# Tiles 4 to 7 normed in quarters and transposed by VectorE, with the scales spread by one masked product for four tiles

## The chip, the cores and the metric

One core of a Trainium2 chip runs the whole program. The metric is device time in microseconds (us), of whole executions; beside it one execution was taken by the hardware profiler, and its span, its rows and its waits are what the texts below read. PE is TensorE, ACT is ScalarE, DVE is VectorE, POOL is GpSimd, and SP (SyncE) issues the DMAs.

## The reference

x has 2048 rows of 640. Its rows are normed to mean 0 and variance 1, and the normed xn goes two ways:

```python
xn = _layernorm(x, axis=-1)
s = _A_ref(xn, A_wqkv, A_wo)          # 32 heads of 20; each row attends to 8 rows, 2 apart
g = _silu(_B_ref(xn, B_w_gate, B_w_up, B_w_down))   # ((xn Wg) * (xn Wu)) Wd, width 1536
return x + s * g
```

## The kernel before

The rows are cut into 16 tiles of 128 partitions. Tile s holds every 16th row, and tiles 0 to 7 are the even columns, 8 to 15 the odd ones, so that the dilated window of a row lies in neighbouring tiles of the same parity. All products are done in three passes of a fast fp32 type: each operand is split into a high part (a copy by ACT) and a low part (raw minus high, by DVE or POOL), and `mm3` adds high·high, high·low and low·high.

The order of the work is written out by hand: each engine executes its instructions in the order in which the program issues them, and waits at an instruction until its operands and its buffers are free. The stages are:

1. **Norming and transposing x** (to about 70 us). The products need xn with its 640 columns on the partitions, in `xT`: four chunks of four tiles, each with a high and a low part. `moments` gives mean and variance of a tile (two bn_stats and one bn_aggr on DVE), `rstd` the reciprocal root (Sqrt on ACT, L191, then a Newton step on DVE, L194 to L206), `apply` the normed tile (L209).
   - Tiles 0 to 7: `norm`, then `trans` (L223): five 128x128 transposes on PE against the identity, a high copy by ACT from PSUM (L224) and two low parts by DVE (L225).
   - Tiles 8 to 15: `moments` reads the tile as it lies; then the tile is loaded again (`load_xq`) from `xq`, a layout prepared on the host in which the 32-row and 160-column blocks are already exchanged, so that a transpose within 32x32 blocks, which DVE can do, finishes the job. In that layout a partition holds four quarters that belong to four different rows. Therefore the scales have to be spread: `spread` multiplies the table of means and scales of eight tiles (`mro`) by four selection matrices (`sel`, L240), and ACT copies the result out of PSUM (`mrq`, L241). `trans_odd` then applies four quarters (L209), transposes (L249), lets ACT make the high part (L252) and leaves the low part (L254) to be done behind the next tile's transpose, or by `low_parts`.
2. **Units and gate_ups** (to about 560 us). A unit u is a group of heads at one parity: `qkv(u, i)` is the product of tile i of that parity by the unit's weights, in one of four PSUM banks of tag q, copied by ACT into `q_t` and `kv_t` (L289, L290). Two kv buffers alternate. When a unit's eight blocks are done, `attention(u)` joins the list `running`. It is a generator; `advance` takes as many of its steps as a credit of estimated DVE time allows, and `drain(u - 2)` takes all that is left before unit u begins. Its steps are pairs of product and sum for the logits (L321, L324), the softmax with an exponent on ACT (L333), weighted sums (L342, L350, L353). `gate_up(f, ch)` is a block of 128 gate columns by chunk ch: a half g and a half u, 15 products each, in PSUM tags g and u with two banks each. ACT copies g to `gs` (L389). Then, while attention is running, DVE multiplies u by gs (L400), issued amid the next piece; while none is running, ACT copies u (L402) and POOL multiplies (L403), at once. An h_scr DMA stores the result. Units 0 and 1 and gate_ups (0, 0) to (1, 3) are written out singly (L650 to L700); from unit 2 on, three or four gate_ups follow each unit.
3. **Output projection, then the down projection** with a Strassen-like scheme and the gated sum (from about 560 us).

The weights of a gate block are split in the same way, the high part by ACT (L85), the low part by POOL (L86), one block ahead.

The order of the program around the change, from about 20 us on: qkv(0, 2), qkv(0, 3), second part of gate_up(0, 0), transposes of tiles 4 and 5, gate_up(1, 0) with the transposes of tile 6 between its halves, those of tile 7, qkv(0, 4), qkv(0, 5), gate_up(0, 1) with the spread between its halves, qkv(0, 6), qkv(0, 7), gate_up(1, 1), unit 1 (eight blocks), gate_up(0, 2), (1, 2), (0, 3), (1, 3), unit 2.

Of the kernel before, what the change touches and what calls it, by code (L numbers as in the profile page):

```python
# [13 lines left out]
AF = mybir.ActivationFunctionType  # L14
# [5 lines left out]
P = 128  # L20
S, D, F = 2048, 640, 1536
H, DH = 32, 20
W, DIL = 8, 2
NT = S // P
NE = NT // DIL
# [4 lines left out]
TPC = CH // P  # L30
# [4 lines left out]
QB = 32  # L35
NQ = P // QB
QC = D // NQ
# [13 lines left out]
def kernel(  # L51
# [11 lines left out]
    nc = tc.nc  # L63
# [11 lines left out]
    def st(shape, tag, bufs, dt=F32):  # L75
        cnt[0] += 1
        return sb.tile(shape, dt, tag=tag, bufs=bufs, name=f"{tag}_{cnt[0]}")

    def pt(shape, tag, bufs):
        cnt[0] += 1  # L80
        return ps.tile(shape, F32, tag=tag, bufs=bufs, name=f"{tag}_{cnt[0]}")
# [37 lines left out]
    def load_wf(f):  # L119
        wf_raw[f] = st([P, KD, 2, P], "wraw", 3)  # L120
        nc.sync.dma_start(wf_raw[f], wgu[f])
# [8 lines left out]
    xt = {}  # L130
# [15 lines left out]
    xc = st([P, NE, D], "xc", NCH)  # L146
# [5 lines left out]
    ident = st([P, P], "ident", 1)  # L152
# [27 lines left out]
    def moments(s0, n, mv=None):  # L180
        stats = st([P, n, 2, 6], "stats", 2)
        mv = st([P, n, 2], "mv", 2) if mv is None else mv
        for i in range(n):
            for a in range(2):
                nc.vector.bn_stats(stats[:, i, a, :], xt[s0 + i][:, a * HALF:(a + 1) * HALF])
            nc.vector.bn_aggr(mv[:, i, :], stats[:, i])
        return mv

    def rstd(var, out, n):
        r = st([P, 4, NE], "rstd", 2)[:, :, :n]  # L190
        nc.scalar.activation(r[:, 0, :], var, AF.Sqrt, bias=eps_t)  # L191
        step = 1 if n <= 2 else n
        for i in range(0, n, step):
            nc.vector.tensor_scalar_add(r[:, 1, i:i + step], var[:, i:i + step], EPS)  # L194
        nc.vector.reciprocal(r[:, 2, :], r[:, 0, :])
        if step == 1:
            for i in range(n):
                ve, a, b = (r[:, k, i:i + 1] for k in (1, 2, 3))
                nc.vector.tensor_scalar(b, a, a, ve, op0=ALU.mult, op1=ALU.mult)
                nc.vector.tensor_scalar(b, b, -0.5, 1.5, op0=ALU.mult, op1=ALU.add)  # L200
                nc.vector.tensor_scalar(out[:, i:i + 1], b, a, None, op0=ALU.mult)
            return
        nc.vector.tensor_mul(r[:, 3, :], r[:, 2, :], r[:, 2, :])
        nc.vector.tensor_mul(r[:, 3, :], r[:, 3, :], r[:, 1, :])
        nc.vector.tensor_scalar(r[:, 3, :], r[:, 3, :], -0.5, 1.5, op0=ALU.mult, op1=ALU.add)
        nc.vector.tensor_mul(out, r[:, 3, :], r[:, 2, :])  # L206

    def apply(y, m, r):
        nc.vector.tensor_scalar(y, y, m, r, op0=ALU.subtract, op1=ALU.mult)  # L209

    def norm(s0, n, mv=None):
        mv = moments(s0, n) if mv is None else mv
        r = st([P, n], "r", 2)
        rstd(mv[:, :, 1], r, n)
        for i in range(n):
            apply(xt[s0 + i], mv[:, i, 0:1], r[:, i:i + 1])

    def trans(s):
        hi, lo = xT_tile(s)
        for k0, k1 in ((0, 4), (4, KD)):  # L220
            p = pt([P, k1 - k0, P], "q", 4)
            for k in range(k0, k1):
                nc.tensor.transpose(p[:, k - k0, :], xt[s][:, k * P:(k + 1) * P], ident)  # L223
            nc.scalar.activation(hi[:, k0:k1, :], p, AF.Copy)  # L224
            nc.vector.tensor_sub(lo[:, k0:k1, :], p, hi[:, k0:k1, :].bitcast(F32))  # L225

    mvo = st([P, NE, 2], "mvo", 1)
    mro = st([P, 2, NE], "mro", 1)  # L230
    mrq = st([P, NQ, 2, NE], "mrq", 1)

    def load_xq(s, n, t):
        nc.sync.dma_start(t, xq[:, s - NE:s - NE + n, :])

    def spread():

        p = pt([P, NQ, 2, NE], "q", 4)
        for a in range(NQ):
            nc.tensor.matmul(p[:, a], sel[:, a], mro, start=True, stop=True)  # L240
        nc.scalar.activation(mrq, p, AF.Copy)  # L241

    halves = []

    def trans_odd(s):
        for a in range(NQ):
            apply(xt[s][:, a * QC:(a + 1) * QC], mrq[:, a, 0, s - NE:s - NE + 1], mrq[:, a, 1, s - NE:s - NE + 1])
        y = st([P, KD, P], "ot", 2)
        nc.vector.transpose(y.rearrange("p k (q i) -> p k q i", i=QB),  # L249
                            xt[s].rearrange("p (q k j) -> p k q j", q=NQ, j=QB))  # L250
        hi, lo = xT_tile(s)
        nc.scalar.activation(hi, y, AF.Copy)  # L252
        low_parts()
        halves.append(lambda: nc.vector.tensor_sub(lo, y, hi.bitcast(F32)))  # L254

    def low_parts():
        while halves:
            halves.pop(0)()
# [22 lines left out]
    def qkv(u, i, parts=ALL3):  # L281
        g, r = UN[u]
        c = GROUPS[g] * DH
        p = pt([P, 3 * c], "q", 4)
        hi, lo = xT[(r * NE + i) // TPC]
        t0 = (i % TPC) * P
        a, b = (hi[:, :, t0:t0 + P], lo[:, :, t0:t0 + P]), wq[g]
        mm3(p, [([t[:, k, :] for t in a], [t[:, k, :] for t in b]) for k in range(KD)], parts)
        nc.scalar.activation(kv_t[u][:, :, W - 1 + i, :], p[:, c:].rearrange("p (a c) -> p a c", a=2), AF.Copy)  # L289
        nc.scalar.activation(q_t[u][:, i, :], p[:, :c], AF.Copy)  # L290
        for i0, i1 in ((1, 5), (5, NE)):
            if i == i1 - 1:
                for p0, p1 in ((0, 112), (112, 127)):
                    nc.sync.dma_start(kv_t[u][p0 + 1:p1 + 1, :, i0 - 1:i1 - 1, :],
                                      kv_t[u][p0:p1, :, W - 1 + i0:W - 1 + i1, :])
# [83 lines left out]
    def gate_up(f, ch, between=(), amid=(), part=None):  # L379
        if part is None:  # L380
            pp = [pt([P, CH], "g", 2), pt([P, CH], "u", 2)]
            c = slice(0, CH)
        else:
            pp, c = part, slice(CH // 2, CH)
        gate_up_half(f, ch, 0, pp[0], c)
        for act in amid:
            act()
        gs = st([P, CH], "gs", 2)
        nc.scalar.activation(gs, pp[0], AF.Copy)  # L389
        for act in between:  # L390
            act()
        share = (c.stop - c.start) / CH
        finish_piece()
        advance(PACE * 3.25 * share)
        gate_up_half(f, ch, 1, pp[1], c)

        def finish():
            hs = st([P, CH], "hs", 2)
            if running:
                nc.vector.tensor_mul(hs, pp[1], gs)  # L400
            else:
                nc.scalar.activation(hs, pp[1], AF.Copy)  # L402
                nc.gpsimd.tensor_mul(hs, hs, gs)  # L403
            nc.sync.dma_start(h_scr[ch * TPC:(ch + 1) * TPC, :, f, :].rearrange("t p c -> p t c"),
                              hs.rearrange("p (t c) -> p t c", c=P))

        unfinished.append(finish)
        if not running:
            finish_piece()
        advance(PACE * 3.25 * share)  # L410
# [239 lines left out]
    nc.gpsimd.memset(mask, 0.0)  # L650
    for i in range(NE - 1):
        nc.gpsimd.memset(mask[:, i, :W - 1 - i], MASKED)
    sel = st([P, NQ, P], "sel", 1)
    nc.gpsimd.tensor_copy(sel.rearrange("p q (b i) -> p q b i", i=QB),
                          ident.rearrange("p (q i) -> p q i", i=QB).unsqueeze(2).to_broadcast([P, NQ, NQ, QB]))
    norm(4, 4)
    qkv(0, 2)
    qkv(0, 3)
    gate_up(0, 0, part=part0)
    trans(4)  # L660
    trans(5)
    moments(8, 2, mvo[:, 0:2])
    gate_up(1, 0, amid=(lambda: trans(6),))
    moments(10, 2, mvo[:, 2:4])
    load_xq(8, 4, xc[:, 4:8])
    trans(7)
    load_wf(2)
    qkv(0, 4)
    qkv(0, 5)
    moments(12, 2, mvo[:, 4:6])  # L670
    moments(14, 2, mvo[:, 6:8])
    load_xq(12, 3, xa)
    load_xq(15, 1, xd)
    nc.vector.tensor_copy(mro[:, 0, :], mvo[:, :, 0])
    rstd(mvo[:, :, 1], mro[:, 1, :], NE)
    gate_up(0, 1, amid=(spread,))
    trans_odd(8)
    trans_odd(9)
    qkv(0, 6)
    trans_odd(10)  # L680
    qkv(0, 7)
    trans_odd(11)
    gate_up(1, 1, amid=(lambda: trans_odd(12),))
    trans_odd(13)
    begin_unit(1)
    for i in range(8):
        if i == 3:
            running.append((0, attention(0)))
        if i == 2:
            load_wq(1, ((0, 3), (3, 5)))  # L690
            low_parts()
        if i < 2:
            trans_odd(14 + i)
        qkv(1, i)
        advance(PACE * 1.9)
    running.append((1, attention(1)))
    split_wq(1, nc.gpsimd)
    gate_up(0, 2)
    gate_up(1, 2)
    gate_up(0, 3)  # L700
    split_wf(2, nc.gpsimd)
# [156 lines left out]
```

## Time and profile before

| what | us |
|---|---|
| median of 3 runs | 787.61 (787.55 to 787.96) |
| the profiled execution's own time | 787.72 |
| its span in the profile | 785.8 |

The profile page gives each engine's busy time, and a busy time in 40 slices of the span. A row of the view in order of time has the start, the length in us, the engine, the line, the operation, what it writes and reads, its shape, and how many instructions are merged; square brackets name an idle stretch ahead of it and what ended it. A row of the view of waits has the total, the count and the longest. A row of the view by stages has the stretch, the busy us of each engine, the granted clock of PE, and the DMA share. PE's instructions overlap by their fill, so the length of a product is read from start to start.

### The profile page before, as it was taken

The numbers are of one execution on the slowest core, as the hardware profiler recorded it, in microseconds if no ns is written. First come the engines' busy times: TensorE is split into PE (matmuls) and PEld (weight loads), VectorE is DVE, ScalarE is ACT, GpSimd is POOL, SyncE is SP. The second block draws the span as 40 slices with busy tenths as digits, with TensorE's granted clock in tenths as the row PEclk, the third lists the DMA queues.
The fourth block names the chain that finished last, engine by engine and source line by source line (L and its number), as shares of the span: only waits on it lengthen the run. The fifth ranks groups of instructions, "written<-read, shape, count | busy, mean of one in ns | idle before, by whom it ended". The sixth has DMA issues, their size and how long they took to land.

```text
span 785.8 us, 11227 instructions
## 1 busy us (share of the span) xinstructions
PE 778.8 (99%) x4456; PEld 709.7 (90%) x4456; DVE 659.0 (84%) x660; ACT 234.7 (30%) x536; POOL 147.3 (19%) x110
## 2 busy tenths in 40 slices
PE   8999999999999999999999999999999999999997
PEld 6989898889898898899898989888899999999997
DVE  6889899999999979997999999992177667787775
ACT  5334211121112111311221202012366564444442
POOL 5201211022013200410231000112468600000000
PEclk9999999999999999999999999999999999999999
DMA  8272122141132322404033132332797574555534
GB/s 308 80 230 76 41 63 69 48 123 48 50 85 87 96 71 61 118 27 112 28 105 86 58 86 58 102 107 66 164 269 212 165 274 138 195 205 189 181 101 135
DMA packets 81661, 92.68 MB, mean 118 GB/s; under 512 B 23032, under 2 KB 63304, under 8 KB 81480
## 3 DMA queue, kind: packets, MB, share of 16 engines
q1 hardware_dynamic: 81608, 91.96, 38.2%
q8 instruction: 35, 0.57, 0.3%
q14 instruction: 18, 0.15, 0.1%
HBM read 54.53 MB, written 28.31 MB: 105 GB/s over the span
## 4 chain that ended last, share of the span: by engine, by line
PE 99%; DVE 0%; ACT 0%; issue 0%; POOL 0%; POOLq 0%
PE q L95 36%; PE u L95 21%; PE g L95 21%; PE q L598 11%; PE u L598 5%; PE g L598 3%; PE q L157 1%; PE q L223 1%; ACT xc L224 0%; PE q L240 0%; DVE xc L225 0%; DVE q L584 0%; DVE q L585 0%; ACT q L579 0%; POOL ident masks.py:199 0%
## 5 line engine op out<-in xcount | busy, mean ns | idle before, releaser
L95 PE MATMUL u<-xc,wf 128*128 128x512 f32 (+1 forms) x735 | 176.2, 391 | 0.0
L95 PE MATMUL g<-xc,wf 128*128 128x512 f32 (+1 forms) x735 | 176.1, 390 | 0.0
L95 PEld LDWEIGHTS u<-xc,wf 128*128 128x128 f32 x735 | 135.8, 188 | 32.1
L95 PEld LDWEIGHTS g<-xc,wf 128*128 128x128 f32 x735 | 135.4, 188 | 30.9
L95 PE MATMUL q<-wqh,xc 128*128 128x300 f32 (+1 forms) x960 | 159.7, 309 | 1.4 <-DVE xc L225 0.8
L95 PEld LDWEIGHTS q<-wqh,xc 128*128 128x128 f32 x960 | 146.0, 188 | 3.9 <-ACT xc L224 1.4
L321 DVE TENSOR_TENSOR t<-q,kv 128x1600 f32<-128x1600 f32 (+1 forms) x48 | 97.7, 2036 | 10.0 <-DMA kv<-kv 10.0
L342 DVE TENSOR_TENSOR t<-e,kv 128x1600 f32<-128x1600 f32 (+1 forms) x48 | 97.5, 2051 | 1.1
L86 POOL TENSOR_TENSOR wf<-wraw,wf 128x256 fp32r<-128x256 f32 (+2 forms) x22 | 48.5, 2223 | 248.0 <-ACT wf L85 229.8
L324 DVE TENSOR_REDUCE lg<-t 128x80 f32<-128x1600 f32 (+1 forms) x48 | 92.6, 1930 | 1.2
L389 ACT ACTIVATE gs<-g 128x512 f32<-128x512 f32 x48 | 28.7, 598 | 205.9 <-PE g L95 190.8
L95 PE MATMUL q<-wql,xc 128*128 128x300 f32 (+1 forms) x480 | 86.0, 309 | 0.0
L350 DVE TENSOR_TENSOR t<-t,t 128x1600 f32<-128x1600 f32 (+1 forms) x36 | 80.3, 2231 | 1.1
L95 PEld LDWEIGHTS q<-wql,xc 128*128 128x128 f32 x480 | 74.3, 188 | 0.0
L289 ACT ACTIVATE kv<-q 128x200 f32<-128x200 f32 (+1 forms) x96 | 33.4, 348 | 133.0 <-PE q L95 133.0
L598 PE MATMUL q<-xc,wf 128*128 128x320 f32 x432 | 67.3, 309 | 0.0
L598 PEld LDWEIGHTS q<-xc,wf 128*128 128x128 f32 x432 | 64.3, 188 | 0.0
L86 POOL TENSOR_TENSOR wql<-wraw,wqh 128x300 fp32r<-128x300 f32 (+4 forms) x15 | 33.2, 2238 | 142.8 <-ACT wqh L85 137.6
L95 PE MATMUL q<-wf,wf 128*128 128x320 f32 x156 | 35.7, 310 | 0.0
L400 DVE TENSOR_TENSOR hs<-u,gs 128x512 f32<-128x512 f32 x39 | 26.7, 683 | 0.7 <-issue 0.7
L95 PEld LDWEIGHTS q<-wf,wf 128*128 128x128 f32 x156 | 26.1, 189 | 0.0
L86 DVE TENSOR_TENSOR wf<-ot,wf 128x640 fp32r<-128x640 f32 x13 | 14.8, 1137 | 12.8 <-ACT wf L85 12.8
(161 smaller groups left out, 892.2 us busy)
## 6 DMA issues: line engine op xcount, KB each, us to landing
h_scr<-hs SPq DMA_DIRECT2D x48, 256.0 KB, 2.3
wraw<-in_wgu SPq DMA_DIRECT2D x12, 640.0 KB, 5.1
t<-h_scr SPq DMA_DIRECT2D x8, 768.0 KB, 7.2
hs<-s_scr SPq DMA_DIRECT2D x16, 320.0 KB, 4.3
gs<-in_x SPq DMA_DIRECT2D x16, 320.0 KB, 4.7
wraw<-h_scr SPq DMA_DIRECT2D x12, 384.0 KB, 6.0
out<-q SPq DMA_DIRECT2D x14, 320.0 KB, 3.4
wraw<-in_wd SPq DMA_DIRECT2D x12, 320.0 KB, 4.9
```

What stands on the lines that cost most here:

```text
L86: eng.tensor_sub(lo, raw, hi.bitcast(F32))
L95: nc.tensor.matmul(acc, a, b, start=first and n == 0, stop=last and n == len(runs) - 1)
L157: nc.tensor.matmul(pt([P, 3, P], "q", 4), ident, ident.unsqueeze(1).to_broadcast([P, 3, P]), start=True, stop=True)
L223: nc.tensor.transpose(p[:, k - k0, :], xt[s][:, k * P:(k + 1) * P], ident)
L289: nc.scalar.activation(kv_t[u][:, :, W - 1 + i, :], p[:, c:].rearrange("p (a c) -> p a c", a=2), AF.Copy)
L321: nc.vector.tensor_mul(t, q.rearrange("p i c -> p (i c)").unsqueeze(1).to_broadcast([P, 2, NE * c]), places(0, j))
L324: nc.vector.tensor_reduce(out=lg[:, :, j:j + 2].rearrange("p n a -> p a n"), in_=heads(t), op=ALU.add, axis=AX.X)
L342: nc.vector.tensor_mul(heads(t), pw, heads(places(1, j)))
L350: nc.vector.tensor_add(acc, acc, t)
L389: nc.scalar.activation(gs, pp[0], AF.Copy)
L400: nc.vector.tensor_mul(hs, pp[1], gs)
L598: nc.tensor.matmul(p, y[:, i, k], wd_t[name][k][:, l], start=new and r == 0, stop=r == len(runs) - 1, skip_group_check=True)
```

## The change

Tiles 4 to 7 go the way of the odd tiles. `xq` now holds twelve tiles (4 to 15). The scales are made and spread for four tiles at a time, in three tables (tiles 4, 8, 12). `sel` becomes one 128x128 matrix, and the choice of the quarter is made by a mask: DVE multiplies the table, repeated four times, by `quarter` (one column of ones for each quarter of the partitions), and a single product by `sel` spreads it. The order around it is written anew: unit 0's eight blocks stand together ahead of gate_up(0, 1), unit 1's blocks are cut in two by gate_up(0, 2), and attention(0) joins behind gate_up(0, 2) instead of at the fourth block of unit 1.

```diff
-    mvo = st([P, NE, 2], "mvo", 1)
-    mro = st([P, 2, NE], "mro", 1)
-    mrq = st([P, NQ, 2, NE], "mrq", 1)
+    stat = {s: (st([P, TPC, 2], "mvo", 3), st([P, 2, TPC], "mro", 3)) for s in range(TPC, NT, TPC)}
+    own, spread_t = {}, {}
+
+    def moments_q(s, n):
+        s0 = s // TPC * TPC
+        moments(s, n, stat[s0][0][:, s - s0:s - s0 + n])
 
     def load_xq(s, n, t):
-        nc.sync.dma_start(t, xq[:, s - NE:s - NE + n, :])
-
-    def spread():
-
-        p = pt([P, NQ, 2, NE], "q", 4)
+        nc.sync.dma_start(t, xq[:, s - TPC:s - TPC + n, :])
+
+    def scales(s0):
+        mv, mr = stat[s0]
+        nc.vector.tensor_copy(mr[:, 0, :], mv[:, :, 0])
+        rstd(mv[:, :, 1], mr[:, 1, :], TPC)
+        own[s0] = st([P, NQ, 2, TPC], "own", 2)
+        nc.vector.tensor_mul(own[s0], mr.unsqueeze(1).to_broadcast([P, NQ, 2, TPC]),
+                             quarter.unsqueeze(2).unsqueeze(3).to_broadcast([P, NQ, 2, TPC]))
+
+    def spread(s0):
+
+        p = pt([P, NQ, 2, TPC], "q", 4)
+        nc.tensor.matmul(p, sel, own[s0], start=True, stop=True)
+        spread_t[s0] = st([P, NQ, 2, TPC], "mrq", 2)
+        nc.scalar.activation(spread_t[s0], p, AF.Copy)
+
+    halves = []
+
+    def trans_q(s):
+        m, i = spread_t[s // TPC * TPC], s % TPC
         for a in range(NQ):
-            nc.tensor.matmul(p[:, a], sel[:, a], mro, start=True, stop=True)
-        nc.scalar.activation(mrq, p, AF.Copy)
-
-    halves = []
-
-    def trans_odd(s):
-        for a in range(NQ):
-            apply(xt[s][:, a * QC:(a + 1) * QC], mrq[:, a, 0, s - NE:s - NE + 1], mrq[:, a, 1, s - NE:s - NE + 1])
+            apply(xt[s][:, a * QC:(a + 1) * QC], m[:, a, 0, i:i + 1], m[:, a, 1, i:i + 1])
...
-    sel = st([P, NQ, P], "sel", 1)
-    nc.gpsimd.tensor_copy(sel.rearrange("p q (b i) -> p q b i", i=QB),
-                          ident.rearrange("p (q i) -> p q i", i=QB).unsqueeze(2).to_broadcast([P, NQ, NQ, QB]))
-    norm(4, 4)
+    quarter, sel = st([P, NQ], "quarter", 1), st([P, P], "sel", 1)
+    nc.gpsimd.memset(quarter, 0.0)
+    for a in range(NQ):
+        nc.gpsimd.memset(quarter[a * QB:(a + 1) * QB, a:a + 1], 1.0)
+    nc.gpsimd.tensor_add(sel[:, :QB], ident[:, :QB], ident[:, QB:2 * QB])
+    for a in range(2, NQ):
+        nc.gpsimd.tensor_add(sel[:, :QB], sel[:, :QB], ident[:, a * QB:(a + 1) * QB])
+    nc.gpsimd.tensor_copy(sel[:, QB:].rearrange("p (b i) -> p b i", i=QB),
+                          sel[:, :QB].unsqueeze(1).to_broadcast([P, NQ - 1, QB]))
+    for i in range(TPC):
+        moments_q(4 + i, 1)
+        load_xq(4 + i, 1, xc[:, i:i + 1])
+    scales(4)
+    moments_q(8, 2)
     qkv(0, 2)
     qkv(0, 3)
     gate_up(0, 0, part=part0)
-    trans(4)
-    trans(5)
-    moments(8, 2, mvo[:, 0:2])
-    gate_up(1, 0, amid=(lambda: trans(6),))
-    moments(10, 2, mvo[:, 2:4])
-    load_xq(8, 4, xc[:, 4:8])
-    trans(7)
+    spread(4)
+    trans_q(4)
+    trans_q(5)
+    gate_up(1, 0)
     load_wf(2)
+    trans_q(6)
+    trans_q(7)
     qkv(0, 4)
     qkv(0, 5)
-    moments(12, 2, mvo[:, 4:6])
-    moments(14, 2, mvo[:, 6:8])
+    low_parts()
+    moments_q(10, 2)
+    load_xq(8, 4, xc[:, 4:8])
+    scales(8)
+    qkv(0, 6)
+    qkv(0, 7)
+    moments_q(12, 4)
     load_xq(12, 3, xa)
     load_xq(15, 1, xd)
-    nc.vector.tensor_copy(mro[:, 0, :], mvo[:, :, 0])
-    rstd(mvo[:, :, 1], mro[:, 1, :], NE)
-    gate_up(0, 1, amid=(spread,))
-    trans_odd(8)
-    trans_odd(9)
-    qkv(0, 6)
-    trans_odd(10)
-    qkv(0, 7)
-    trans_odd(11)
-    gate_up(1, 1, amid=(lambda: trans_odd(12),))
-    trans_odd(13)
+    gate_up(0, 1, amid=(lambda: spread(8),))
+    scales(12)
+    trans_q(8)
+    spread(12)
+    trans_q(9)
+    trans_q(10)
+    trans_q(11)
+    gate_up(1, 1)
     begin_unit(1)
-    for i in range(8):
-        if i == 3:
-            running.append((0, attention(0)))
-        if i == 2:
+    trans_q(12)
+    for i in range(TPC):
+        if i == 1:
             load_wq(1, ((0, 3), (3, 5)))
-            low_parts()
-        if i < 2:
-            trans_odd(14 + i)
+        qkv(1, i)
+    trans_q(13)
+    trans_q(14)
+    trans_q(15)
+    gate_up(0, 2)
+    low_parts()
+    running.append((0, attention(0)))
+    for i in range(TPC, NE):
         qkv(1, i)
         advance(PACE * 1.9)
     running.append((1, attention(1)))
     split_wq(1, nc.gpsimd)
-    gate_up(0, 2)
     gate_up(1, 2)
```

More of the change, by code (lines that the diff above doesn't have):

```diff
@@ L836 @@
     arrays["xb"] = lay(arrays["x"].reshape(S, NQ, KD, QB).transpose(0, 2, 1, 3).reshape(S, D))
-    odd = arrays["x"].reshape(NQ, QB, NE, DIL, NQ, QC)[:, :, :, 1]
-    arrays["xq"] = lay(odd.transpose(3, 1, 2, 0, 4).reshape(P, NE, D))
+    quarters = arrays["x"].reshape(NQ, QB, NE, DIL, NQ, QC).transpose(3, 4, 1, 2, 0, 5).reshape(DIL, P, NE, D)
+    arrays["xq"] = lay(np.concatenate([quarters[0][:, TPC:], quarters[1]], axis=1))
     q3 = np.asarray(A_wqkv).reshape(D, 3, D)
```

## The prediction

> **What bounds the kernel now.** I read the page's first part, then the waits of TensorE (PE), then the busy time by stage, then the order of time around the change.
>
> ```profile
> PE 778.8 (99%) x4456; PEld 709.7 (90%) x4456; DVE 659.0 (84%) x660; ACT 234.7 (30%) x536; POOL 147.3 (19%) x110
> ```
> ```profile
> PE q L157 <- POOL ident masks.py:199: 1.4, 1, 1.4
> PE q L95 <- DVE xc L225: 0.8, 1, 0.8
> PE q L95 <- ACT xc L224: 0.6, 1, 0.6
> ```
> ```profile
> 110.00:150.00 40.00, 40.00 (x209) 34.51 (x209) 38.95 (x29) 6.81 (x18) 4.18 (x1) 1.00 0.25 73
> ```
>
> PE is busy 99% of 785.8 us; its waits sum to 2.8 us and all lie in the first 21 us. So PE's own work is the time, and a change pays only by what it takes off PE's queue or costs only by what makes PE wait. The stage row warns of the second: from 110 to 150 us VectorE (DVE) is busy 38.95 of 40 us. DVE is almost as full as PE there, so a DVE that is put behind does not catch up quickly. The 84% of the first row hides this.
>
> **What PE loses and gains in products.** Tiles 4 to 7 are now transposed on PE (L223), between the halves of a gate_up:
>
> ```profile
> 27.81 1.25 PE L223 MATMUL q<-ident,xc 128*128 128x128 f32 x10
> ...
> 32.41 0.71 PE L223 MATMUL q<-ident,xc 128*128 128x128 f32 x5
> ...
> 36.44 0.71 PE L223 MATMUL q<-ident,xc 128*128 128x128 f32 x5
> 36.91 0.94 PE L95 MATMUL q<-wqh,xc 128*128 128x300 f32 x5
> ...
> 44.62 0.96 PE L240 MATMUL q<-mro,sel 128*128 128x16 f32 x8
> 45.43 3.74 PE L95 MATMUL u<-xc,wf 128*128 128x512 f32 x15
> 49.01 0.86 PE L95 MATMUL q<-wqh,xc 128*128 128x300 f32 x5
> ...
> 60.13 0.86 PE L95 MATMUL q<-wqh,xc 128*128 128x300 f32 x5
> ...
> 76.62 3.66 PE L95 MATMUL g<-xc,wf 128*128 128x512 f32 x15
> ...
> 87.11 3.67 PE L95 MATMUL u<-xc,wf 128*128 128x512 f32 x15
> ...
> 104.61 0.85 PE L95 MATMUL q<-wqh,xc 128*128 128x300 f32 x5
> ```
>
> I use start-to-start times, since the ends overlap. An undisturbed gate_up half takes 3.50 (76.62 to 87.11 is three). From 27.81 to 36.91 are 9.10 us with two halves (7.00) in them: the 20 transposes and their switches cost **2.10**, all of which goes. The old spread (L240) takes 45.43 - 44.62 = 0.81 and the half behind it 3.58, so 0.89 for four products in eight records. The new kernel has three products of 128x32, one for each four tiles: two records (0.20) and a switch (0.08) each, 0.84 in all. A product of this shape isn't in the trace; bounds are 0.1 (one record) and 0.8 (all eight). Sum of PE's own work: **-2.15 us**.
>
> **The new wait.** The moments are now turned into scales three times, and the third time stands at an awkward place. On ScalarE (ACT) the order is: spread copy, gs copy and hs copy of gate_up(0, 1), then the Sqrt of scales(12). With no attention running, that hs copy reads u of gate_up(0, 1) as soon as it ends. On PE, spread(12) is the very next thing after that u. So PE ends u, and then waits for hs copy, Sqrt, DVE's Newton step and masked product, in a row. All of PE's queue stands behind it.
>
> ```profile
> 42.76 0.30 ACT L191 ACTIVATE rstd<-mvo,eps 128x8 f32<-128x8 f32 x1 [0.96 <-DVE mvo L186]
> ...
> 49.21 0.60 ACT L402 ACTIVATE hs<-u 128x512 f32<-128x512 f32 x1 [2.87 <-PE u L95]
> ```
> ```profile
> 43.09 0.20 DVE L195 RECIPROCAL rstd<-rstd 128x8 f32<-128x8 f32 x1
> ...
> 43.94 0.17 DVE L206 TENSOR_TENSOR mro<-rstd 128x8 f32<-128x8 f32 x1
> ```
>
> hs starts 0.20 after u gives way (49.21 against 49.01) and takes 0.60, the Sqrt 0.30, reciprocal to last multiply 1.02 (43.09 to 44.11), the masked product about 0.2 (nearest is the 0.17 of L206; it has 32 elements for 8), and PE's restart about 0.2: **+2.5 us**, with ends 2.2 and 3.0. DVE itself is in time: its moments are done before u ends, so nothing on DVE shortens this. The two other spreads don't wait, since their Sqrts stand well ahead.
>
> The Trainium skill speaks against such a gap: "TensorE: Matmul & The Clock Gate", Part 1, has the array's clock drop to half after an idle window of about 3.4 us, and its closing table asks for no gap over about 3 us. By that rule an estimate of 2.5 stays just below; what crossing it would cost is the third rival.
>
> **Tiles 4 to 7 in time?** DVE, per tile: four applies, transpose, low part.
>
> ```profile
> 26.46 2.18 DVE L209 TENSOR_SCALAR xc<-xc,mv,r 128x640 f32<-128x640 f32 x4
> ...
> 51.84 1.17 DVE L209 TENSOR_SCALAR xc<-xc,mrq 128x160 f32<-128x160 f32 x4
> ...
> 57.21 1.17 DVE L209 TENSOR_SCALAR t<-t,mrq 128x160 f32<-128x160 f32 x4
> ```
>
> A tile costs 2.68 (51.84 to 57.21 is two). The scales of tiles 4 to 7 are there at about 26.5, as today; moments of tiles 8 and 9 follow, and a POOL product that holds the applies up, to about 30. Low part 6 would then be done near 30 + 4 x 2.68 = 40.7. PE, at 28.1 after the spread, does 7.0 of gate_up(1, 0) and two blocks of qkv (16.49 for eight, 60.13 to 76.62, so 2.06 each) and wants it in the third pass of the next, near 40.6. I take **+0.1** (0 to 0.8). The reloads of x in quarters lie beside this: SP issues each behind its tile's moments, 3 us and more before use. The rest I cost at nothing: POOL builds sel and the quarter mask in nine small steps in place of one copy, behind the same memsets and some 4 us before the first spread reads them; DVE's extra work on these tiles (2.68 against 0.55 for an apply and two low parts) lies beside gate_up(1, 0) as just counted; load_wq(1) moves up on SP by less than a gate_up and is read only after unit 1. Start of unit 1: 60.13 - 2.15 + 2.5 + 0.1 = 60.6, 0.45 later than now, though tiles 4 to 7 have left PE.
>
> **The attention that starts later.** attention(0) now joins after gate_up(0, 2) instead of at the fourth block of unit 1, and its exponent comes on ACT behind the gs copy of gate_up(0, 3) instead of gate_up(1, 2): one gate_up, 7.0 us, later.
>
> ```profile
> 87.37 0.60 ACT L389 ACTIVATE gs<-g 128x512 f32<-128x512 f32 x1 [6.40 <-PE g L95]
> 87.99 1.28 ACT L333 ACT_TABLE_LOAD   x1
> 89.28 0.47 ACT L333 ACTIVATE e<-lg 128x320 f32<-128x320 f32 x1
> ```
> ```profile
> 91.28 3.56 DVE L342 TENSOR_TENSOR t<-e,kv 128x1600 f32<-128x1600 f32 x2
> ...
> 99.06 4.48 DVE L350 TENSOR_TENSOR t<-t,t 128x1600 f32<-128x1600 f32 x1
> 103.58 1.82 DVE L342 TENSOR_TENSOR t<-e,kv 128x1600 f32<-128x1600 f32 x1
> ...
> 143.19 0.68 DVE L400 TENSOR_TENSOR hs<-u,gs 128x512 f32<-128x512 f32 x1
> ...
> 179.57 0.68 DVE L400 TENSOR_TENSOR hs<-u,gs 128x512 f32<-128x512 f32 x1
> 180.17 3.16 DVE L353 TENSOR_TENSOR o<-t 128x800 f32<-128x800 f32 x1
> ...
> 293.48 1.83 DVE L321 TENSOR_TENSOR t<-q,kv 128x1600 f32<-128x1600 f32 x1 [4.34 <-DMA kv<-kv]
> ```
> ```profile
> 145.59 3.67 PE L95 MATMUL u<-xc,wf 128*128 128x512 f32 x15
> ...
> 183.07 3.65 PE L95 MATMUL u<-xc,wf 128*128 128x512 f32 x15
> ...
> 198.25 1.53 PE L95 MATMUL q<-wqh,xc 128*128 128x300 f32 x10
> ...
> 200.31 1.76 PE L95 MATMUL q<-wqh,xc 128*128 128x300 f32 x10
> ```
> ```profile
> 178.17 4.31 POOL L86 TENSOR_TENSOR wf<-wraw,wf 128x1280 fp32r<-128x1280 f32 x1 [5.77 <-ACT wf L85]
> ```
>
> Measured from PE, DVE's weighted sums (91.28 now) start 7.0 later; one gate product fewer on DVE (gate_up(0, 2) now goes to ACT and POOL) gives 0.6 back: DVE is **6.4 us further behind PE** when attention(1) begins. What is late next:
>
> - kv of unit 2 takes attention(0)'s buffer. Its last read ends at 103.58 + 1.82 = 105.40 now, so at 112.85 then (7.0 + 0.45). PE starts unit 2 at 105.06 and can fill four q banks, to 113.3; the copies out of the first need some 0.5. Just met: **+0.1** (0 to 1).
> - The gate product at 143.19 frees the u bank that PE needs at 145.59: 1.7 us to spare. The new order has it two weighted steps (about 3.7) earlier in DVE's queue, so it comes 6.4 - 3.7 = 2.7 later, 1.0 too late; less the 0.1 just paid, **+0.9** (0 to 1.5).
> - The one at 179.57 has 183.07 - 180.25 = 2.8 to spare. DVE is now 5.4 behind, less 3.7: 1.7 later, 1.1 left. But a POOL split stretches two-input DVE work that meets it: L350 at 99.06 took 4.48 instead of 1.83, L353 at 180.17 took 3.16 instead of 0.99. The split at 178.17 is tied to PE; it now meets a step ahead of the gate product, +2.2 to 2.65: **+1.3** (0 to 2).
> - Unit 4 has 0.23 of stall today (1.76 instead of 1.53), as ACT waits for an exponent amid the blocks; that exponent now comes two blocks later: **-0.23**.
> - Units 5 and 6 have gate products and exponents of the same kind: **+0.3** (0 to 1.5). By 293.48 DVE waits 4.34 us for DMA, which takes up what lag is left; behind it nothing changes.
>
> **Sum**: -2.15 + 2.5 + 0.1 + 0.1 + 0.9 + 1.3 - 0.23 + 0.3 = **+2.8 us**. The profiled execution took 787.72 us (785.8 span and 1.9 around it), 0.1 over the median of 787.61. Forecast: **790.5 us**.
>
> **Rivals.**
>
> 1. *Not slower: the lag on DVE is absorbed.* If the splits miss the gate products and the 6.4 us are nearer 4, no u bank is late. Then only the wait at the third spread and the saved products remain: -2.15 + 2.5 + 0.1 - 0.23 = +0.2, 787.9. It decides once the lag is under 3.7 + 1.7 = 5.4 us. For it: the margins are 1.7 and 2.8, and gate products stand earlier. Against: the exponent's place behind gate_up(0, 3) is fixed in ACT's order.
> 2. *Faster: the third spread doesn't hold PE*, and no lag costs: -2.15 - 0.23, 785.3. It needs the Sqrt to pass the hs copy; ACT's order has it the other way round.
> 3. *Slower still: the clock.* If PE's gap costs it its full rate, the half that follows runs slow. The first products of the span show the size:
>
> ```profile
> 1.37 5.49 PE L157 MATMUL q<-ident 128*128 128x384 f32 x8 [1.37 <-POOL ident masks.py:199]
> ...
> 7.55 0.81 PE L157 MATMUL q<-ident 128*128 128x384 f32 x2
> ```
>
> 0.69 each against 0.41, 1.7 times; a half of 3.50 would take 2.4 more: 792.9. Against: the granted clock is 1.00 in every stage that I read; gaps of 0.8 are the longest in the trace after the start.
>
> **How the numbers follow.** About 0.2% (1.6 us) is what a measurement of this kernel can tell from no change, so slower begins at 789.2. Forecast 0.62 (own range 788.9 to 792.2, a little of it under 789.2), absorbed lag 0.25, faster 0.05, clock 0.08. The range takes in the absorbed lag below and most of the bounds above: 787.4 to 792.7. Faster 0.05, same 0.26, slower 0.69.
>
> **What would show it.** PE's waits name DVE's masked product once, at about 51 us and for 2.5; if absent, rival 2. No L223 on PE after 20 us; unit 1 at 60.6. The exponent of attention(0) at some 96 to 97. PE stalls ahead of u halves near 146 and 184 put down to the gate product; if absent, rival 1 holds. The granted clock under 1.00 after 51 us would speak for rival 3. A slow landing of the quartered x, or DVE's tiles 4 to 7 later than I have them, would make the prediction wrong from another side: PE waits at 35 to 43 us.

## The result: slower by 0.8%, and the profile after

The changed kernel takes 793.87 us (median of 6 runs, 792.33 to 795.31) against 787.74 for the kernel before on the same chips: a ratio of 1.0076, 95% interval [1.0065, 1.0087]. The forecast was 790.5 with a range of 787.4 to 792.7: the sign was right, the size was not. The execution in the profile took 793.85 us with a span of 792.1, against 787.72 and 785.8 before, so 6.3 us of span are to be found.

The page's first part and two rows of PE's waits, after:

```profile
PE 779.7 (98%) x4434; PEld 709.4 (90%) x4434; DVE 666.2 (84%) x682; ACT 235.1 (30%) x536; POOL 145.7 (18%) x119
```
```profile
PE q L250 <- DVE own L244: 3.1, 1, 3.1
PE u L95 <- DVE hs L412: 1.5, 2, 1.2
```

22 records have left PE, as they should. Two long waits are new. The first is the one that the prediction named, once, for DVE's masked product; it is 3.1 long, not 2.5. The second is the gate product that frees a u bank, twice. Yet PE's busy time has risen by 0.9 although it does less: some of its products have become slower. PE in order of time, after:

```profile
27.82 0.30 PE L250 MATMUL q<-own,sel 128*128 128x32 f32 x2
27.96 3.75 PE L95 MATMUL g<-xc,wf 128*128 128x512 f32 x15
31.55 3.66 PE L95 MATMUL u<-xc,wf 128*128 128x512 f32 x15
...
47.00 0.30 PE L250 MATMUL q<-own,sel 128*128 128x32 f32 x2
47.14 3.74 PE L95 MATMUL u<-xc,wf 128*128 128x512 f32 x15
53.96 0.38 PE L250 MATMUL q<-own,sel 128*128 128x32 f32 x2 [3.08 <-DVE own L244]
54.18 5.29 PE L95 MATMUL g<-xc,wf 128*128 128x512 f32 x15
59.31 3.67 PE L95 MATMUL u<-xc,wf 128*128 128x512 f32 x15
62.82 0.85 PE L95 MATMUL q<-wqh,xc 128*128 128x300 f32 x5
...
149.24 3.76 PE L95 MATMUL u<-xc,wf 128*128 128x512 f32 x15 [0.28 <-DVE hs L412]
...
188.32 3.76 PE L95 MATMUL u<-xc,wf 128*128 128x512 f32 x15 [1.24 <-DVE hs L412]
```

A spread takes 0.14 from its start to that of the half behind it, and that half 3.59 instead of 3.50. The half u at 47.14, behind such a spread too, gives way at 50.72, and the third spread starts at 53.96: **3.24 us** of wait. The half g behind it lasts from 54.18 to 59.31, 5.13 where 3.58 is right for one behind a spread: **1.55 us** more. Unit 1 starts at 62.82 (60.13 before, 60.6 predicted).

What PE waited for, in the order of each engine: ACT, DVE, POOL of the kernel after.

```profile
50.91 0.60 ACT L414 ACTIVATE hs<-u 128x512 f32<-128x512 f32 x1 [2.89 <-PE u L95]
51.41 0.29 ACT L191 ACTIVATE rstd<-mvo,eps 128x4 f32<-128x4 f32 x1
```
```profile
51.73 0.18 DVE L195 RECIPROCAL rstd<-rstd 128x4 f32<-128x4 f32 x1 [2.29 <-ACT rstd L191]
51.94 0.98 DVE L203 TENSOR_TENSOR rstd<-rstd 128x4 f32<-128x4 f32 x1
52.95 0.16 DVE L204 TENSOR_TENSOR rstd<-rstd 128x4 f32<-128x4 f32 x1
...
53.62 0.19 DVE L244 TENSOR_TENSOR own<-mro,quarter 128x32 f32<-128x32 f32 x1
```
```profile
51.64 1.26 POOL L415 TENSOR_TENSOR hs<-hs,gs 128x512 f32<-128x512 f32 x1 [14.43 <-ACT hs L414]
```

The order is the predicted one: copy of u, Sqrt, Newton step, masked product, spread. What the prediction left out is the row of L203: a multiply of four columns takes 0.98, where the next one (L204) takes 0.16. It ends at 52.92, and POOL's gate product, which the same hs copy released, ends at 52.90. The 0.8 us too many of the wait lie there. The reciprocal ahead of it has one input and was not held (0.18), though POOL's product ran beside it; the same L203 of scales(8), at 44.17 with POOL idle, took 0.16. This agrees with the Trainium skill, "SBUF — State Buffer", "Who interferes with whom": DVE and GpSimd share a pair of ports under an exclusive lock, and a DVE instruction with two inputs in SBUF contends with a GpSimd instruction that reads SBUF.

The view by stages shows the slow half; the last three columns are granted clock, DMA share and GB/s; after:

```profile
54.00:55.00 1.00, 1.00 (x5) 0.85 (x6) 0.97 (x5) 0.00 (x0) 0.00 (x0) 0.77 0.83 249
55.00:56.00 1.00, 1.00 (x4) 0.81 (x3) 1.00 (x3) 0.18 (x1) 0.00 (x0) 0.50 0.03 10
...
58.00:59.00 1.00, 1.00 (x6) 0.82 (x5) 1.00 (x4) 0.51 (x1) 0.00 (x0) 1.00 0.00 0
```

From about 54.5 to 58.0 PE ran at half its clock. That is the third rival of the prediction, which had 0.08.

Further on, the exponent of attention(0) and the step of DVE that waits for it, after:

```profile
99.06 0.47 ACT L345 ACTIVATE e<-lg 128x320 f32<-128x320 f32 x1
```
```profile
99.57 0.49 DVE L347 TENSOR_REDUCE sm<-e 128x40 f32<-128x320 f32 x1 [3.78 <-ACT e L345]
```

It comes 9.8 later than before (89.28): 7.0 for one gate_up, as predicted, and 2.7 for the later start of unit 1. From there DVE is behind PE, and in the stretch of the prediction's stage row PE now has holes (39.67 of 40 busy, DVE 38.88):

```profile
110.00:150.00 40.00, 39.67 (x211) 34.21 (x210) 38.88 (x28) 7.46 (x22) 4.42 (x1) 1.00 0.20 59
```

A last, small difference is in the chain of work: from unit 1 to unit 7, a unit's eight blocks take 16.59, waits apart, where the kernel before has 16.49; the units of six heads take 19.84 in both. Unit 4, after:

```profile
192.09 16.59 PE q L95 x120
```

### The profile page after: what moved, and what is told of

Read it like the earlier page. It is cut to its first block, busy times and chain, and to the rows that moved or that the text cites. A ratio compares the mean times of both kernels' runs of the same rounds, so it can differ in the third digit from the quotient of the medians.

```text
span 792.1 us, 11227 instructions
## 1 busy us (share of the span) xinstructions
PE 779.7 (98%) x4434; PEld 709.4 (90%) x4434; DVE 666.2 (84%) x682; ACT 235.1 (30%) x536; POOL 145.7 (18%) x119
## 4 chain that ended last, share of the span: by engine, by line
PE 86%; DVE 9%; issue 2%; ACT 1%; DMA 1%; SPq 0%; DVEq 0%; ACTq 0%
PE q L95 32%; PE g L95 18%; PE u L95 18%; PE q L610 11%; PE u L610 5%; PE g L610 3%; DVE t L354 3%; DVE t L333 2%; DVE lg L336 2%; DVE t L362 2%; DVE hs L412 1%; DMA wraw<-in_wqkv 1%; SPq L106 0%; DVE e L349 0%; DVE sm L347 0%
## 5 line engine op out<-in xcount | busy, mean ns | idle before, releaser
L333 DVE TENSOR_TENSOR t<-q,kv 128x1600 f32<-128x1600 f32 (+1 forms) x48 | 99.6, 2075 | 7.2 <-DMA kv<-kv 7.2
L354 DVE TENSOR_TENSOR t<-e,kv 128x1600 f32<-128x1600 f32 (+1 forms) x48 | 102.7, 2152 | 1.1
L86 POOL TENSOR_TENSOR wf<-wraw,wf 128x256 fp32r<-128x256 f32 (+2 forms) x22 | 43.6, 2000 | 241.6 <-ACT wf L85 241.6
L362 DVE TENSOR_TENSOR t<-t,t 128x1600 f32<-128x1600 f32 (+1 forms) x36 | 75.3, 2092 | 1.1
L86 POOL TENSOR_TENSOR wql<-wraw,wqh 128x300 fp32r<-128x300 f32 (+4 forms) x15 | 35.3, 2374 | 140.9 <-ACT wqh L85 140.8
L415 POOL TENSOR_TENSOR hs<-hs,gs 128x512 f32<-128x512 f32 x10 | 12.9, 1290 | 82.6 <-ACT hs L414 45.1
```

What stands on the lines that cost most here:

```text
L86: eng.tensor_sub(lo, raw, hi.bitcast(F32))
L333: nc.vector.tensor_mul(t, q.rearrange("p i c -> p (i c)").unsqueeze(1).to_broadcast([P, 2, NE * c]), places(0, j))
L354: nc.vector.tensor_mul(heads(t), pw, heads(places(1, j)))
L362: nc.vector.tensor_add(acc, acc, t)
```

## The experiments

Theory A, from the profiles: the loss is the third wait (its Sqrt stands on ACT behind the hs copy), the clock that falls because PE has been idle, and the stalls of a late exponent. Theory D: the 0.10 of each unit of five heads is the place of the weights in SBUF, which the change moved by 192 bytes. The rivals are named in the texts on record. Each kernel is compared with the kernel before on its own chip.

### Scales of tile 12 ahead of gate_up(0, 1)

```diff
-    gate_up(0, 1, amid=(lambda: spread(8),))
     scales(12)
+    gate_up(0, 1, amid=(lambda: spread(8),))
```

> The changed kernel with scales(12) issued ahead of gate_up(0, 1), so that its Sqrt stands ahead of the hs copy on ACT. Theory A (the third spread's wait costs 3.3 us, the slow clock behind it 1.6, and DVE's lag from the late exponent another 2 by itself): the wait and the 0.76 clock go, gate_up(1, 1) takes 3.50 a half, unit 1 starts near 57.9 instead of 62.8, the two stalls ahead of u halves (0.3 and 1.2) stay, about 788.9. Rival B (DVE is late only because tiles 8 to 15 start 3 us late behind that wait): the stalls go as well, about 786.8.

Measured: 789.21 us, ratio 1.0021 [1.0011, 1.0031], span 787.3. PE, and DVE's multiply, of this kernel:

```profile
50.73 0.38 PE L250 MATMUL q<-own,sel 128*128 128x32 f32 x2
50.94 3.74 PE L95 MATMUL g<-xc,wf 128*128 128x512 f32 x15
54.52 3.66 PE L95 MATMUL u<-xc,wf 128*128 128x512 f32 x15
```
```profile
49.53 0.16 DVE L203 TENSOR_TENSOR rstd<-rstd 128x4 f32<-128x4 f32 x1
```

One line moved takes some 4.5 us off (1.6 over the kernel before instead of 6.1). The wait is all but gone, the half g behind the spread takes 3.58, and L203, with no POOL product beside it, 0.16. The two stalls for the gate product remain (1.5 in PE's waits), though PE reaches them almost 5 us earlier: so they don't come from the wait. Theory A holds, and its rival, by which the stalls would have gone too, falls.

### The wait filled with products

Four products whose result nobody reads are put on PE ahead of the third spread; the wait for the scales stays.

```diff
     trans_q(8)
+    for _ in range(4):
+        idle_product()
     spread(12)
```

> The changed kernel with four unused products of the identity (0.8 us each) put on PE ahead of the third spread, so that PE works through the wait. Theory A (the slow half after the wait is the granted clock, and the clock falls because PE stood idle): the spread still comes at about 54, but the clock stays 1.00 and the half after it takes 3.50 instead of 5.13; 792.2, and the spread of 3 us between executions gets small. Rival C (the half is slow for another reason, such as the DMA traffic of that moment): 5.13 again and 793.9.

Measured: 792.93 us, ratio 1.0067 [1.0052, 1.0082]. PE of this kernel:

```profile
51.11 2.74 PE L157 MATMUL q<-ident 128*128 128x384 f32 x8
54.36 0.38 PE L250 MATMUL q<-own,sel 128*128 128x32 f32 x2 [0.51 <-DVE own L244]
54.57 3.74 PE L95 MATMUL g<-xc,wf 128*128 128x512 f32 x15
58.15 3.66 PE L95 MATMUL u<-xc,wf 128*128 128x512 f32 x15
```

The spread is as late behind its predecessor as ever, but the half behind it takes 3.58 and the granted clock stays 1.00 in this stage. This one execution doesn't settle it, since the fourth experiment's kept its clock with the wait unfilled. But the four runs of this kernel lie within 0.5 us of one another, where the six of the changed kernel lie within 3.0. And in the profiles of all eleven kernels, as long as PE has products left, the clock falls three times: twice behind this gap of 3.08 us, and once behind one of 2.48 at quite another place (the eighth experiment). So it is PE's idleness that brings the clock down, and not the weights, the DMA or DVE's load at that place.

### Attention(0) advanced at once

```diff
     running.append((0, attention(0)))
+    advance(4.0)
     for i in range(TPC, NE):
```

Steps worth 4 us of DVE are issued ahead of unit 1's fifth block, so that the exponent gets on ACT ahead of the gs copy that held it.

> The changed kernel with 4 us more credit for attention(0) when it joins, so that its exponent stands behind the gs copy of gate_up(1, 2) as before the change. Theory A: DVE's weighted sums start about 6 us earlier; the stalls of unit 2's blocks (0.3), of the u half at 149 (0.45) and of that at 188 (1.4) go; the wait at the third spread and the slow clock stay; about 791.7. Rival B: the stalls stay, 793.9.

Measured: 792.04 us, ratio 1.0058 [1.0043, 1.0073]: 4.4 us over the kernel before, against 6.1 for the changed kernel. The two intervals overlap, so the time alone shows little, but the rows do. The exponent starts at 94.28, and PE's waits name no gate product any more; each gate half from unit 1 on takes 3.50, and unit 2 no longer waits (16.59). The third wait is still there, and in the profiled execution the clock fell for longer than in the profile of the changed kernel. PE and stages of this kernel:

```profile
53.39 0.61 PE L250 MATMUL q<-own,sel 128*128 128x32 f32 x2 [3.08 <-DVE own L244]
53.81 6.48 PE L95 MATMUL g<-xc,wf 128*128 128x512 f32 x15
60.13 3.66 PE L95 MATMUL u<-xc,wf 128*128 128x512 f32 x15
```
```profile
53.00:54.00 1.00, 0.61 (x3) 0.64 (x4) 0.94 (x5) 0.00 (x0) 0.00 (x0) 0.51 0.79 247
```

Here the half g takes 6.32, 2.74 too many; the clock stays at half until nearly 60. With that the stalls of the changed kernel (2.36 in all, below), which are all gone here, are put down to the exponent's place.

### The weights at their former address

A table of 192 bytes in each partition, which nobody reads, is allocated, so that the weights of the units lie where they lay before.

```diff
     own, spread_t = {}, {}
+    nc.gpsimd.memset(st([P, 48], "pad", 1), 0.0)
```

> The changed kernel with an unused buffer of 192 bytes a partition, which puts wqh, wql and what lies behind them at the addresses that they have before the change. Theory D (the qkv blocks of the five-head units take 16.59 instead of 16.49 us for eight because of where the weights lie): 16.49 again, 0.6 us less over all, 793.2. Rival E (it has another cause, such as the clock): 16.59 and 793.9.

Measured: 793.49 us, ratio 1.0073 [1.0058, 1.0088]. PE in order of time and the chain (unit 4) of this kernel:

```profile
53.94 0.38 PE L251 MATMUL q<-own,sel 128*128 128x32 f32 x2 [3.08 <-DVE own L245]
54.15 3.74 PE L95 MATMUL g<-xc,wf 128*128 128x512 f32 x15
57.73 3.67 PE L95 MATMUL u<-xc,wf 128*128 128x512 f32 x15
```
```profile
190.66 16.49 PE q L95 x120
```

The units of five heads are back at 16.49, but for unit 2 with its wait (17.07): the 0.10 hangs on the address (Theory D). Why this address is slower isn't settled. In time the effect, 0.7, is lost in the scatter of the runs (791.75 to 794.71). The other rows say where that scatter is from: the wait is 3.08 to the hundredth as in the changed kernel, and yet this execution kept its clock (3.58).

### The kernel before with a late exponent

```diff
             running.append((0, attention(0)))
+            advance(-6.5)
```

The kernel before, with none of the change; attention(0) is held back by 6.5 us of credit, which puts its exponent behind the gs copy of gate_up(0, 3).

> The kernel before with nothing changed but 6.5 us less credit for attention(0) when it joins, which puts its exponent behind the gs copy of gate_up(0, 3), as the change does. Theory A (the late exponent alone makes DVE's lag): PE stalls appear at unit 2's blocks (0.3), ahead of the u halves near 146 and 184 (0.4 and 1.4), and unit 4's 0.2 goes; about 789.6. Rival B (the tiles' late start is needed for it): 787.6.

Measured: 790.17 us, ratio 1.0029 [1.0018, 1.0041]. A row of PE's waits and one in order of time:

```profile
PE u L95 <- DVE hs L400: 1.7, 2, 1.4
```
```profile
185.35 3.76 PE L95 MATMUL u<-xc,wf 128*128 128x512 f32 x15 [1.40 <-DVE hs L400]
```

The same two stalls, in the same places, without a tile moved. Unit 2 takes 16.70 and unit 4 16.49 (16.72 before): the kv wait comes and the stall of unit 4 goes, as in the changed kernel. The late exponent alone is worth some 2.2 to 2.6 us (by the spans and by the medians); DVE's additional work on tiles 4 to 7 isn't needed for it.

### The three cures together

The edits of the first, the third and the fourth experiment in one kernel.

> The changed kernel with the three cures together: scales(12) ahead of gate_up(0, 1), 4 us more credit for attention(0), and the buffer of 192 bytes. If the four causes found so far are all there is, what is left of the change is the work taken off PE (about 1.9 us less, with 0.3 of wait left at the third spread) and 0.2 of a stall in unit 4 that goes: 785.7. If the transposes on DVE cost something that these cures don't touch, it stays at or above the 787.6 of the kernel before.

Measured: 787.66 us, ratio 0.9998 [0.9989, 1.0007]. Expected was 785.7, so 2 us are missing. PE and DVE of this kernel:

```profile
177.84 3.66 PE L95 MATMUL g<-xc,wf 128*128 128x512 f32 x15
182.78 3.76 PE L95 MATMUL u<-xc,wf 128*128 128x512 f32 x15 [1.28 <-DVE hs L413]
```
```profile
177.66 4.46 DVE L355 TENSOR_TENSOR t<-e,kv 128x1600 f32<-128x1600 f32 x1
182.05 0.68 DVE L413 TENSOR_TENSOR hs<-u,gs 128x512 f32<-128x512 f32 x1
```

Unit 2 starts at 102.87, 1.74 ahead of before: the gain is there. At 177.84 to 182.78 it is given back, 4.94 for 3.50. PE has gained, DVE has not, so DVE is behind PE again, and a weighted step ahead of the gate product takes 4.46 for 1.82, while POOL splits weights (from 176.43, for 4.01). That is 1.44 of the 2 us; another 0.44 lies behind DVE's last instruction, where this kernel has 3.15 to the end of its span and the kernel before 2.71.

### The third spread amid gate_up(1, 1)

The third and the fourth edit as above; in place of the first, the spread is put between the halves of the next gate_up.

```diff
-    spread(12)
     trans_q(9)
     trans_q(10)
     trans_q(11)
-    gate_up(1, 1)
+    gate_up(1, 1, amid=(lambda: spread(12),))
```

> As the run before, but the third spread is moved instead of the scales: it stands between the halves of gate_up(1, 1), 3.5 us later on PE, and scales(12) stays where the change has it. The wait was 3.1, so it should be covered: no wait at any spread, clock 1.00, 785.4. If the wait is longer than a half, a rest of it is seen.

Measured: 789.31 us, ratio 1.0020 [1.0011, 1.0029]; 785.4 was expected. PE of this kernel:

```profile
67.13 0.96 PE L95 MATMUL q<-wqh,xc 128*128 128x300 f32 x5 [0.90 <-DVE xc L267]
67.92 3.66 PE L95 MATMUL g<-xc,wf 128*128 128x512 f32 x15
```
The spread no longer holds PE, but DVE does: it still stands idle for the Sqrt (2.28), and now PE overtakes it and waits for the low parts of tiles 8 to 11 in unit 1. Its four blocks, started at 57.94, take 9.98 for 8.25; and one stall for a gate product, of 1.7, is left near 184. Moving the reader later doesn't help where DVE's own start is what is late; moving the Sqrt earlier does.

### The cures, and the weight split one gate_up later

On the kernel with the three cures: the split of the next gate block's weights, amid gate_up(3, 1), is put amid gate_up(3, 2).

```diff
-        gate_up(f, ch, (lambda: split_wf(f + 1, nc.gpsimd),) if ch == 1 else ())
+        gate_up(f, ch, (lambda: split_wf(f + 1, nc.gpsimd),) if ch == (2 if f == 3 else 1) else ())
```

> The three cures together, and the split of the weights of f = 4, which ACT and POOL did amid gate_up(3, 1), done amid gate_up(3, 2). With the three cures alone PE still loses 1.44 us ahead of the u half at 182.78: the gate product at 182.05 stands on DVE behind a weighted step of 4.46 us (1.82 where no split runs beside it), beside the split on POOL at 176.43. Theory A (a POOL split that meets the two-input steps of the late attention is what makes that gate product late): the split now starts on POOL near 180, behind that step, the step takes 1.8 to 2.6, the product comes near 179.5 to 180.3, the wait of 1.3 goes, and the time is 787.66 - 1.4 = 786.2, 0.9983 of before. Theory B (DVE is late there by its own backlog, and a split anywhere near stretches another step by as much): the stall is found again at the next gate product or ahead of unit 4's copies, and the time stays at 787.7.

Measured: **786.02 us, ratio 0.9973 [0.9964, 0.9983]**: faster than both kernels. The profiled execution was the longest of the twelve, 789.16: its first weights came late, so its rows stand 3.1 later than those of the kernel with the three cures. PE at that place, and the stage behind it:

```profile
11.05 1.83 PE L95 MATMUL q<-wqh,xc 128*128 128x300 f32 x6 [2.48 <-ACT wqh L85]
```
```profile
12.00:13.00 1.00, 1.00 (x6) 1.00 (x6) 0.96 (x3) 0.00 (x0) 0.00 (x0) 0.50 0.89 300
```

A gap of 2.48 us was enough to halve the clock here. PE and DVE around the stall:

```profile
180.92 3.66 PE L95 MATMUL g<-xc,wf 128*128 128x512 f32 x15
184.42 3.65 PE L95 MATMUL u<-xc,wf 128*128 128x512 f32 x15
```
```profile
180.75 1.83 DVE L355 TENSOR_TENSOR t<-e,kv 128x1600 f32<-128x1600 f32 x1
182.49 0.68 DVE L413 TENSOR_TENSOR hs<-u,gs 128x512 f32<-128x512 f32 x1
```

The step takes 1.83, the gate product is in time, the half 3.50. POOL's split starts at 186.45, later than expected, well behind this gate product. So the stall was the meeting with the split and not DVE's backlog by itself.

### The later split in the kernel before

The same line changed in the kernel before, and nothing else.

> Only the later split of the weights of f = 4, in the kernel before. If the 786.02 that the changed kernel reached with all four cures is a gain of the transposes taken off PE, this kernel, which still has them on PE, gains nothing: before shows no wait of PE at that place, so 787.6 to 787.8 (ratio 1.000). If the later split is good by itself, because less of the attention's work is stretched, it comes to 787.0 or under, and the gain isn't the change's.

Measured: 787.31 us, ratio 1.0000 [0.9991, 1.0008]. By itself the later split brings nothing that can be told from no change: the median lies 0.4 under that of its kernel before, between the two expectations. So most of the 0.27% of the kernel above is the change's own. By the rows of the kernel with the cures, unit 2 starts 1.74 earlier for the work taken off PE, and unit 4's stall of 0.23 is gone; some 0.5 of that is lost again behind the last instruction.

## Why the prediction was right in sign and wrong in size

Its terms, in its own order, against the two profiles (start to start):

| step | predicted | measured |
|---|---|---|
| PE's own products | -2.15 | -2.24 |
| wait at the third spread | +2.5 | +3.24 |
| slow clock behind it | 0 (third rival: 2.4) | +1.55 |
| low part of tile 6 | +0.1 | +0.12 |
| kv of unit 2 | +0.1 | +0.31 |
| gate product, first | +0.9 | +0.55 |
| gate product, second | +1.3 | +1.50 |
| unit 4's stall | -0.23 | -0.23 |
| units 5 and 6 | +0.3 | 0 |
| address of the weights | not seen | +0.7 |
| from 563 us on, on PE | 0 | +0.12 |
| behind the last instruction | 0 | +0.59 |
| sum | +2.8 | +6.2 (span: 6.3) |

The sum was 3.4 short: 1.55 for the clock, 0.74 for the wait, 0.7 for the address of the weights and 0.59 for the end of the span, with small differences both ways.

- **The products** were right. 29.25 us of halves and blocks lie between 27.8 us and unit 1 in both kernels; of the rest, transposes and spread of before were 2.99, the three spreads now are 0.23, 0.22 and 0.30.
- **The step that failed is the new wait**, "+2.5 us, with ends 2.2 and 3.0". Its chain was right link by link up to the Newton step: "reciprocal to last multiply 1.02 (43.09 to 44.11)" was taken from a place where POOL stood still. At the new place the hs copy, which begins the chain, also releases POOL's gate product, and L203 meets it: 0.98 for 0.16. The prediction used this very effect for the 4.48 of L350 further on, but not for an instruction of four columns. The first experiment shows it from the other side (0.16).
- **The clock**, the largest miss, was put at nothing and comes with that step. "By that rule an estimate of 2.5 stays just below": the gap was 3.1 to 3.2, and four of the six runs took 1.5 us or more above the shortest. Nor would 2.5 have been safe, as the gap of 2.48 in the eighth experiment shows. The price of rival 3, 2.4, lies among those measured (1.55 in the profile, 2.74 in the third experiment, none in the fourth), but by some luck: for the first products of the span, from which it was read, the view by stages has a clock of 1.00. Its chance was too small, since it was taken as a case apart and not as what can come with the wait itself.
- **The attention that starts later** was right in mechanism and about right in sum: 2.36 against 2.6 for the kv buffer, the two u banks and units 5 and 6. Rival 1 ("the lag is absorbed") fell, and the third experiment, with the lag taken away, and the fifth, with the lag alone, show both sides of its condition.
- **Costed at nothing and right**: the quartered reloads of x, the nine small steps on POOL, load_wq(1). PE has no wait at 35 to 43 us beyond the 0.12 in the table.
- **Costed at nothing and wrong**: the change moved the unit weights by 192 bytes, 0.10 a unit. And from DVE's last instruction to the end of the span there are 3.30 now and 2.71 before:

```profile
788.31 0.49 DVE L597 TENSOR_TENSOR q<-q,gs 128x320 f32<-128x320 f32 x1
```
```profile
782.60 0.49 DVE L585 TENSOR_TENSOR q<-q,gs 128x320 f32<-128x320 f32 x1
```

  (after, then before). All profiled kernels that have the change show 3.15 to 3.30, and the three without it 2.71 to 2.76. So this isn't chance, but its cause is open; no experiment was made on it.

## What to carry to other kernels

Work taken off a full engine pays only if the one that gets it can keep up: here DVE was busy 38.95 of 40 us, and the gain came out only when, beside the address of the weights, three things had been cleared away (a Sqrt behind a copy, an attention that began late, a POOL split that met a gate product). Where one event releases a chain, look at what else it releases: the neighbour can hold the chain's smallest link. And a wait of PE such as those of 2.48 and 3.08 us here isn't a term of a sum with a width of its own: in some executions it brings the slower clock with it, so the two belong in one case.

## What the runs showed of the hardware that was not expected

- The same gap of 3.08 us on PE (by the row of waits) left the clock alone in one profiled execution, halved it in another and in a third; the half behind it took 3.58, 5.13 and 6.32. A gap of 2.48 at another place halved it as well. By the clock column, slice by slice, the stretches at half clock are 3.42, 6.84 and 3.42 us long. Accordingly the changed kernel's runs go from 792.33 (mean granted clock 0.999) to 795.31 (0.994). The Trainium skill, "TensorE: Matmul & The Clock Gate", Part 1, has the clock go by windows of about 3.4 us that run freely, without regard to the program, and take only half or full rate. The rows agree: 0.50 or 1.00, but for slices in which it changes, for the length of one or two such windows. Yet gaps shorter than one window, 3.08 and 2.48, were enough for the drop here. That the same gap falls differently into the windows from run to run would explain why the clock falls or not; no run shows it.
- A DVE multiply of 128x4 took 0.98 for 0.16 beside a POOL product of 128x512, and ended with it to within 0.02.
- 120 products of 300 columns took 16.59 or 16.49 us, by 192 bytes in the address of their weights.
